# Whole-word float32 products for the first three units of two blocks, and VectorE and ScalarE ordered by hand at the start

## The chip, the cores and the metric

The kernel runs on one core of one Trainium2 chip. The metric is the device time of one execution in microseconds (us), here the median of three runs. TensorE does the matrix products, VectorE and ScalarE the elementwise work, GpSimd (POOL in the profile) more elementwise work, and SyncE's queue (SP) issues the transfers between HBM and the on-chip memory.

## The reference

There are two parts, and only the second one's result is returned. The first is a recurrent attention over 768 steps, for 4 batches of 8 heads of width 48:

```
cur   = u*k_t (outer) v_t
y_t   = r_t . (state + cur)
state = w_t * state + k_t (outer) v_t
```

The second is a feed-forward layer on the 3072 rows of 384 that come out of it: `h = x @ w_in` (384 to 2048), `g = h * cos(h)`, `out = g @ w_out` (2048 to 384). All data are float32.

## The kernel before, in words

The attention is cut into 24 chunks of 128 steps (4 batches, 6 chunks each), and two chunks make a block of 256 rows; `order` takes one chunk of every batch in turn. A chunk j goes through steps with one-letter names in the plan strings: `load` and `lv` (its transfers), `decay` (running products of the decays by two scans on VectorE, then r and k scaled by them), `diag` (the diagonal u terms, on TensorE for the first eight chunks), `a` (scores, masked into `asb` by VectorE), `t` and `s` (transposed k and the new state), `d` (the decayed state), `o` and `p` (the own and the past part of y) and `x` (y rounded into `xT`).

The feed-forward layer works on tiles f of 128 of the 2048 hidden columns, 16 in all. Two tiles make a unit of 512 columns of a PSUM bank (two tiles times 256 rows). For every unit and block `mm1` forms h, `gate` forms g on ScalarE, VectorE and GpSimd, and `mm2`, three units later, adds g times the output weights into the block's accumulators. The products run in float32r, a rounded form. To keep float32 accuracy each operand is split into a rounded high part and a low part (the rest), and a product is made of three passes, high by high, high by low and low by high (`PASSES`): 18 products for a unit's mm1, 12 for its mm2.

The weights come as 64-bit words and are made into float32 by `load_weights`: three casts on ScalarE (L163, L166, L167), a shift and an add on VectorE (L168, L169), the rounding to the high part on ScalarE (a cast at L141) and the low part on VectorE (a subtraction at L144). A tile holds its columns of w_in (kind 0) and rows of w_out (kind 1) side by side, so each of these steps covers 768 columns.

The raw words sit in the space of later tiles' weights (`RING`, five places): a raw transfer can start when the tile in its place has been cast.

The order: `START` is a list of steps for the first units, in which `f` is the transfer of a weight tile, `w` its conversion, `m0` and `m1` the two tiles of the next unit's mm1, and `mm2` the next mm2. `PAIR` says which of blocks 0 and 1 each of the first sixteen units belongs to: three units of block 0, three of block 1, then by turns. TensorE takes its instructions in the written order (`manual_schedule`). On all other engines a planner with its own estimates orders them, the written order being the priority. After `START`, `PLAN` gives a row of steps for every unit. `EARLY` and `LATER` say which engine does each kind of step.

Of the kernel before, what the change touches and what calls it, by code (L numbers as in the profile page):

```python
# [20 lines left out]
C = 128  # L21
# [13 lines left out]
BY_HAND = "P"  # L35
MERGE = 1
# [7 lines left out]
PASSES = ((0, 0), (0, 1), (1, 0))  # L44

LAG = 3
HP = 50
EARLY = dict(whole="p", rkt="v", cd="a", pc0="a", pc1="a", wadd="v", wm="a", whi0="a", whi1="a", ksh="a", gh="a", xh="a", rzh0="p", rzh1="v", r3="v", k3="v", rk="p", ru="p", rf0="v", rf1="v", kn="a", dd="v", rd0="a", rd1="a", rz0="v", rz1="v", ks="v", g0="p", g1="p", x="v", wlo0="v", wlo1="p", qf="s", qt="s", qr="s", qv="s", qx0="s", qx1="s", qo="s")
# [12 lines left out]
START = ["load0 load1 f lv0 decay0 f diag0 a0 lv1 decay1 diag1 a1 w load2 f w o0 x0 decay2 diag2 m0 m1",  # L61
# [10 lines left out]
def rwkv_cos_ffn(ctx: ExitStack, tc: tile.TileContext, tr, tn, tv, u, ut, wts, w, rkw, vst, us, xs, out):  # L72
# [80 lines left out]
    def load_weights(f):  # L153

        bits = raw.pop(f)
        wgt[f] = wt.tile([128, 2, 2, DM], F32R, tag=f"w{f}", name=f"w{f}")
        step = 2 if MERGE else 1
        for kind in range(0, 2, step):
            high, rest = wgt[f][:, kind:kind + step, 0], wgt[f][:, kind:kind + step, 1]
            words = bits[:, kind:kind + step].rearrange("p k (n w) -> p k n w", w=2)  # L160
            hi, lo = words[:, :, :, 1], words[:, :, :, 0]
            h = buf("h", [128, step, DM], I32)
            nc.scalar.activation(h.bitcast(F32), hi.bitcast(F32), AF.Copy, scale=2.0 ** -111)  # L163
            rest_of = buf("rd", [128, step, DM], I32)
            low16 = rest_of.bitcast(I16).rearrange("p k (n q) -> p k n q", q=2)
            nc.scalar.activation(low16[:, :, :, 0], lo.bitcast(U32), AF.Copy, scale=2.0 ** -29)  # L166
            nc.scalar.activation(low16[:, :, :, 1].bitcast(F16), hi.bitcast(F32), AF.Copy, scale=2.0 ** -60)  # L167
# [33 lines left out]
    def att_decay(a):  # L201

        if a["j"] < BY_PE:
            a["rkt"] = buf("rkt", [R, NP, C], F32)
            E["rkt"].tensor_tensor(out=a["rkt"], in0=a["r3"], in1=a["k3"], op=ALU.mult)  # L205
        wp = a["tt"][:, 1024:1024 + W129 + 1]
# [10 lines left out]
        E["r3"].tensor_tensor(out=a["r3"], in0=a["r3"], in1=a["pp"], op=ALU.mult)  # L217
        E["k3"].tensor_tensor(out=a["k3"], in0=a["k3"], in1=ee[:, :, 1:129], op=ALU.mult)
# [35 lines left out]
    def att_scores(a):  # L254
# [5 lines left out]
        for h in range(2):  # L260
            nc.vector.copy_predicated(a["asb", h], mask, pa[h])  # L261
# [91 lines left out]
    def gate(pool, ph, split=True):  # L353
# [7 lines left out]
        if not split:  # L361
            return rr
# [343 lines left out]
```

## Time and profile before

| | |
|---|---|
| median of 3 runs | 545.76 us (545.52 to 547.07) |
| the profiled execution | 547.09 us, its span 545.4 us |
| TensorE (PE) busy | 516.6 us, 95% of the span |
| VectorE (DVE) busy | 368.1 us, 68% |
| ScalarE (ACT) busy | 270.7 us, 50% |
| GpSimd (POOL) busy | 205.0 us, 38% |
| mean granted TensorE clock | 0.995 |

The span is the time from the first to the last instruction of one execution, which is run under the hardware profiler. Busy time counts instructions in progress. A row of the timeline gives the start, the duration and the engine, then the line of the kernel, the operation, what it writes and reads with the shapes, and how many instructions are merged into the row; in brackets stands the idle time of the engine before it and what ended this. PEld is TensorE's weight load. A line can be a helper's (L141 is every copy, L144 every low part).

### The profile page before, as it was taken

The numbers are of one execution on the slowest core, as the hardware profiler recorded it, in microseconds if no ns is written. First come the engines' busy times: TensorE is split into PE (matmuls) and PEld (weight loads), VectorE is DVE, ScalarE is ACT, GpSimd is POOL, SyncE is SP. The second block draws the span as 40 slices with busy tenths as digits, with TensorE's granted clock in tenths as the row PEclk, the third lists the DMA queues.
The fourth block names the chain that finished last, engine by engine and source line by source line (L and its number), as shares of the span: only waits on it lengthen the run. The fifth ranks groups of instructions, "written<-read, shape, count | busy, mean of one in ns | idle before, by whom it ended". The sixth has DMA issues, their size and how long they took to land. (4 is left out here: it accounts for less than half of the span.)

```text
span 545.4 us, 11929 instructions
## 1 busy us (share of the span) xinstructions
PE 516.6 (95%) x4980; PEld 492.9 (90%) x4980; DVE 368.1 (68%) x568; ACT 270.7 (50%) x456; POOL 205.0 (38%) x274
## 2 busy tenths in 40 slices
PE   3668999999899999999999999999999999999996
PEld 3666989989899999999999999999999999999996
DVE  7988999978787477478478478468468664433331
ACT  1778999645343444344444444344344345344542
POOL 4141336653344335335334334334334334323332
PEclk9999999999899999999999999999999999999999
DMA  8984771204370060061061051052032330000000
GB/s 269 277 303 167 240 220 41 77 7 132 117 180 16 30 183 12 30 171 25 30 170 26 30 150 46 30 148 48 29 106 99 131 131 1 31 1 1 30 2 31
DMA packets 16440, 51.38 MB, mean 94 GB/s; under 512 B 1984, under 2 KB 8384, under 8 KB 16384
## 3 DMA queue, kind: packets, MB, share of 16 engines
q1 hardware_dynamic: 16240, 50.49, 30.9%
q8 instruction: 40, 0.66, 0.5%
q14 instruction: 16, 0.13, 0.1%
q10 hardware_dynamic: 144, 0.10, 0.1%
HBM read 45.87 MB, written 4.72 MB: 93 GB/s over the span
## 5 line engine op out<-in xcount | busy, mean ns | idle before, releaser
L144 POOL TENSOR_TENSOR gs<-rr,gs 128x256 fp32r<-128x256 f32 x192 | 159.0, 850 | 228.3 <-ACT gs L141 220.1
L382 PE MATMUL ph<-xT,w 128*128 128x256 f32 x1728 | 225.2, 285 | 6.3 <-ACT w L141 4.8
L382 PEld LDWEIGHTS ph<-xT,w 128*128 128x128 f32 x1728 | 216.5, 192 | 9.8 <-ACT w L141 5.3
L401 PE MATMUL acc<-w,gs 128*128 128x384 f32 x1152 | 218.7, 339 | 1.0 <-DVE rr L360 1.0
L401 PEld LDWEIGHTS acc<-w,gs 128*128 128x128 f32 x1152 | 196.1, 188 | 4.6 <-issue 3.0
L359 ACT ACTIVATE rr<-rr,quarter 128x512 f32<-128x512 f32 x96 | 69.4, 723 | 110.2 <-DVE rr L358 110.0
L358 DVE SCALAR_TENSOR_TENSOR rr<-rr,ph 128x512 f32<-128x512 int32 x96 | 65.5, 682 | 76.2 <-ACT rr L357 63.3
L360 DVE TENSOR_TENSOR rr<-rr,ph 128x512 f32<-128x512 f32 x96 | 65.4, 682 | 46.8 <-ACT rr L359 46.8
L357 ACT ACTIVATE rr<-ph 128x512 int32<-128x512 f32 x96 | 57.1, 595 | 57.6 <-PE ph L382 57.4
L141 ACT CAST gs<-rr 128x512 fp32r<-128x512 f32 x96 | 59.0, 615 | 50.8 <-PE acc L401 40.3
L236 POOL TENSOR_SCALAR_AFFINE_SELECT asb<-cd 128x512 f32<-128x512 f32 x48 | 33.7, 733 | 50.6 <-ACT cd L141 25.6
L261 DVE COPY_PREDICATED asb<-mask,pa 128x512 f32<-128x512 uint8 x48 | 32.9, 735 | 5.8 <-PE pa L259 5.8
L259 PE MATMUL pa<-tt 48*128 48x128 f32 x384 | 32.6, 311 | 1.6 <-ACT ob L414 1.4
L259 PEld LDWEIGHTS pa<-tt 48*128 48x128 f32 x384 | 27.1, 210 | 6.8 <-issue 4.4
L208 DVE TENSOR_TENSOR_SCAN ee<-tt,one_e 112x516 f32<-112x516 f32 x24 | 31.4, 1308 | 1.8 <-DMA tt<-tr 1.8
L213 DVE TENSOR_TENSOR_SCAN tt<-tt,inj 112x516 f32<-112x516 f32 x24 | 31.3, 1303 | 0.1
L141 POOL COPY wholes<-ee 112x4 f32<-112x4 f32 x24 | 10.5, 438 | 54.1 <-DVE ee L208 54.1
L141 ACT COPY past<-dd 48x192 f32<-48x192 f32 x40 | 14.0, 351 | 21.9 <-DVE dd L249 21.3
L224 PEld LDWEIGHTS pc<-u_by_head,rkt 112*128 112x128 f32 x64 | 11.1, 259 | 14.8 <-DVE rkt L205 8.6
L224 PE MATMUL pc<-u_by_head,rkt 112*128 112x2 f32 x64 | 11.3, 299 | 13.6 <-DVE rkt L205 13.1
L217 DVE TENSOR_TENSOR tt<-tt 112x512 f32<-112x512 f32 x24 | 20.0, 833 | 0.1
L229 DVE TENSOR_TENSOR rk<-rk 128x384 f32<-128x384 f32 x16 | 10.9, 680 | 12.4 <-DMA rk<-tn 12.4
(65 smaller groups left out, 346.4 us busy)
## 6 DMA issues: line engine op xcount, KB each, us to landing
tt<-tr SPq DMA_DIRECT2D x22, 674.2 KB, 7.3
raw<-wts SPq DMA_DIRECT2D x16, 768.0 KB, 5.9
rk<-tn SPq DMA_DIRECT2D x16, 384.0 KB, 3.3
v<-tv SPq DMA_DIRECT2D x24, 224.0 KB, 7.0
ww<-w SPq DMA_DIRECT2D x6, 768.0 KB, 4.3
out<-ob SPq DMA_DIRECT2D x23, 192.0 KB, 2.0
tt<-tr SPq DMA_DIRECT2D x4, 224.0 KB, 4.3
tt<-tr SPq DMA_DIRECT2D x2, 226.2 KB, 3.5
```

Source lines behind the costliest of these rows:

```text
L141: (nc.scalar.copy if E[name] is nc.scalar else E[name].tensor_copy)(out=out, in_=in_)
L144: E[name].tensor_tensor(out=out, in0=full, in1=high.bitcast(F32), op=ALU.subtract)
L208: nc.vector.tensor_tensor_scan(out=ee.rearrange("p a t -> p (a t)")[:, ::-1], data0=wp[:, 1:W129 + 1][:, ::-1], data1=one_e.rearrange("p a ...
L236: nc.gpsimd.affine_select(out=asb, in_=col.unsqueeze(2).to_broadcast([C, NP, C]), pattern=[[0, 4], [1, C]], compare_op=ALU.is_equal, fill= ...
L259: nc.tensor.matmul(out=pa[h][:, p], lhsT=a["k3"][rows(h), p], rhs=a["r3"][rows(h), p], start=True, stop=True)
L261: nc.vector.copy_predicated(a["asb", h], mask, pa[h])
L357: nc.scalar.activation(nn, ph, AF.Copy, scale=INV2PI / W_SCALE, bias=0.25)
L358: nc.vector.scalar_tensor_tensor(out=rr, in0=nn, scalar=-2.0 * math.pi * W_SCALE, in1=ph, op0=ALU.mult, op1=ALU.add)
L359: nc.scalar.activation(rr, rr, AF.Sin, scale=1.0 / W_SCALE, bias=quarter)
L360: nc.vector.tensor_tensor(out=rr, in0=rr, in1=ph, op=ALU.mult)
L382: nc.tensor.matmul(out=ph[:, fi], lhsT=wgt[u * FU + fi][:, 0, a, kt * 128:(kt + 1) * 128], rhs=xT[:, b, kt], start=n == 0, stop=n == 3 * K ...
L401: nc.tensor.matmul(out=accs[i][j][:, :DM], lhsT=gs[:, a, fi, j * C:(j + 1) * C], rhs=wgt[u * FU + fi][:, 1, b], start=u == 0 and fi == 0 a ...
```

## The change

- For blocks 0 and 1, a unit of tiles below `WHOLE` (6, so units 0 to 2) forms mm1 by three float32 products per tile, of the whole weight words (`wholly`) and of x as float32 (`xfs`), instead of nine float32r products. The whole words lie in the space of later tiles' weights (8 to 10), x in that of tile 11.
- The split of these six tiles into high and low parts is a step of its own, `part_weights`, for w_in (`z` in the lists) and for w_out (`k`) separately. The high parts are ScalarE casts of 384 columns. The low part of w_in is VectorE's, that of w_out GpSimd's (`wlo0` and `wlo1` in `EARLY`). The split of x (`part_x`, `X`) is a step of its own as well.
- `START` is cut in two. In the first part VectorE and ScalarE also follow the written order, up to unit 2. Steps there can leave their later half for a place of its own: `later` keeps it under a name, and `!name` in the list (or `finish`) writes it out: `r` the f16 cast of a tile, `h` its shift and add, `y` the scaling of r and k by the decays, `c` the masked copies, `g` and `G` the two halves of a gate. In the second part (`START2`) only TensorE is by hand.
- The product r times k for the diagonal of chunks 0 and 1 moves behind the scans. The sine is applied once to a constant at the start.

```diff
-START = ["load0 load1 f lv0 decay0 f diag0 a0 lv1 decay1 diag1 a1 w load2 f w o0 x0 decay2 diag2 m0 m1",
-         "load3 f lv2 w f decay3 diag3 w m0 a2 m1 lv3 w f a3 o1 x2 w f m0 m1 mm2",
...
+START = ["load0 load1 f lv0 f decay0 !y0 diag0 a0 w !r0 lv1 load2 decay1 !y1 diag1 a1 w !r1 f load3 !c0 !h0 !c1 !h1 f w o0 x0 !r2 lv2 f w !r3 m0 m1",
+         "decay2 !y2 !h2 a2 decay3 !g0 !h3 f w !r4 !G0 lv3 m0 m1 f w !r5 !y3 diag3 !c2 a3 !g1 !c3 !h4 !G1 !h5 k0 k1 o1 x2 m0 m1"]
+START2 = ["k0 k1 k2 mm2 m0 m1 w f t0 t1 k3 mm2 m0 m1 s0 w f k4 k5 mm2 m0 m1 X0 z0 z1 w f load4 mm2 t2 t3 m0 m1 X1 z2 z3 w f s1 lv4",
+          "mm2 m0 m1 z4 z5 w f load5 mm2 m0 m1 w f decay4 lv5 mm2 m0 m1 w f diag4 decay5 mm2 a4 m0 m1 w f diag5 mm2 m0 m1 w a5 mm2 m0 m1 w load6 d4 d5",
...
+    nc.scalar.activation(cst.tile([128, 1], F32, name="first_sine"), quarter, AF.Sin)
...
+    def later(key, rest):
+
+        if by_hand[0]:
+            rests[key] = rest
+        else:
+            rest()
...
+    def part_weights(f, kind):
+
+        if f >= WHOLE or (f, kind) in parted:
+            return
+        finish("h%d" % f)
+        parted.add((f, kind))
+        if f not in wgt:
+            wgt[f] = wt.tile([128, 2, 2, DM], F32R, tag=f"w{f}", name=f"w{f}")
+        whole = wholly[f][:, f % 2, kind].bitcast(F32)
+        high, rest = wgt[f][:, kind, 0], wgt[f][:, kind, 1]
+        copy("whi%d" % kind, high, whole)
+        low_part("wlo%d" % kind, rest, whole, high)
...
+    def part_x(i):
+
+        xts[i] = xT = buf("xT", [128, 2, KT, BT], F32R)
+        copy("xh", xT[:, 0], xfs[i])
+        low_part("x", xT[:, 1], xfs[i], xT[:, 0])
...
+            if i < 2 and u * FU + fi < WHOLE:
+                for kt in range(KT):
+                    nc.tensor.matmul(out=ph[:, fi], lhsT=wholly[u * FU + fi][:, fi, 0, kt * 128:(kt + 1) * 128].bitcast(F32),
+                                     rhs=xfs[i][:, kt], start=kt == 0, stop=kt == KT - 1)
+                continue
...
+    with tc.manual_schedule(engines={ET.PE}):
+        by_hand[0] = True
+        with tc.manual_schedule(engines={ET.DVE, ET.Activation}):
+            first_order(START)
+        by_hand[0] = False
+        for key in list(rests):
+            finish(key)
+        first_order(START2)
```

## Rows read from the trace of the kernel before

**Rows 1.** Busy time by stretches: the stretch and its length in us, busy us and count of PE, PEld, DVE, ACT and POOL, then the granted TensorE clock, the DMA share and GB/s.

```profile
36.30:40.20 3.90, 0.00 (x0) 0.00 (x0) 3.90 (x5) 3.90 (x7) 2.49 (x2) 1.00 0.64 224
40.20:53.40 13.20, 10.68 (x107) 8.74 (x108) 11.91 (x18) 11.59 (x16) 2.82 (x3) 1.00 0.52 182
53.40:65.00 11.60, 11.60 (x109) 11.42 (x108) 11.08 (x16) 11.60 (x18) 2.00 (x4) 1.00 0.63 209
65.00:110.00 45.00, 42.96 (x346) 41.41 (x345) 45.00 (x63) 38.52 (x59) 26.75 (x23) 1.00 0.40 122
110.00:140.00 30.00, 29.02 (x329) 27.23 (x327) 24.45 (x38) 13.24 (x26) 13.14 (x17) 1.00 0.26 76
```

**Rows 2.** Timeline of the start, TensorE's first units and the first group of second products (L401).

```profile
25.58 4.19 PE L382 MATMUL ph<-xT,w 128*128 128x256 f32 x18
...
40.22 0.79 PE L382 MATMUL ph<-xT,w 128*128 128x256 f32 x2 [3.94 <-ACT w L141]
...
41.47 1.86 PE L382 MATMUL ph<-xT,w 128*128 128x256 f32 x7 [0.45 <-DVE w L144]
...
53.41 2.27 PE L401 MATMUL acc<-w,gs 128*128 128x384 f32 x12
```

**Rows 3.** The same timeline: ScalarE's three casts of a weight tile, and the load of the sine table.

```profile
14.13 0.90 ACT L163 ACTIVATE h<-raw 128x768 f32<-128x768 f32 x1
...
14.93 1.06 ACT L166 ACTIVATE rd<-raw 128x768 int16<-128x768 uint32 x1
...
15.86 1.06 ACT L167 ACTIVATE rd<-raw 128x768 f16<-128x768 f32 x1
...
33.40 1.28 ACT L359 ACT_TABLE_LOAD   x1
```

**Rows 4.** The same timeline: the masked copies, GpSimd's selects, add, x copies, shift, ScalarE's first gate step, VectorE's low part, VectorE's gate step, the sine and the gate's cast.

```profile
13.73 1.33 DVE L261 COPY_PREDICATED asb<-mask,pa 128x512 f32<-128x512 uint8 x2
...
14.30 1.23 POOL L236 TENSOR_SCALAR_AFFINE_SELECT asb<-cd 128x512 f32<-128x512 f32 x2 [2.14 <-ACT cd L141]
...
17.39 0.95 DVE L169 CUSTOM_DVE_ANT_0 h<-h,rd 128x1536 uint16<-128x1536 uint16 x1
...
20.15 0.83 ACT L141 CAST xT<-py 128x384 fp32r<-128x384 f32 x2
...
24.79 0.53 DVE L168 TENSOR_SCALAR h<-h 128x768 int32<-128x768 int32 x1
...
29.80 0.60 ACT L357 ACTIVATE rr<-ph 128x512 int32<-128x512 f32 x1 [0.56 <-PE ph L382]
30.08 0.94 DVE L144 TENSOR_TENSOR w<-h,w 128x768 fp32r<-128x768 f32 x1
...
30.95 0.67 DVE L358 SCALAR_TENSOR_TENSOR rr<-rr,ph 128x512 f32<-128x512 int32 x1
...
34.69 0.72 ACT L359 ACTIVATE rr<-rr,quarter 128x512 f32<-128x512 f32 x1
...
37.02 0.60 ACT L141 CAST gs<-rr 128x512 fp32r<-128x512 f32 x1
```

**Rows 5.** The issue of the raw transfers of weight tiles 2 and 3 (timeline of the start), and from the list of transfers issued between 7.1 and 7.9 and between 8.4 and 9 us: count, KB each, us from issue to landing.

```profile
7.20 0.71 SPq L151 DMA_DIRECT2D raw<-wts  x1
8.49 0.41 SPq L151 DMA_DIRECT2D raw<-wts  x1
...
raw<-wts SPq DMA_DIRECT2D x1, 768.0 KB, 14.0
...
raw<-wts SPq DMA_DIRECT2D x1, 768.0 KB, 18.5
```

**Rows 6.** Timeline, TensorE's rates: products at 46.97 and 48.31, and float32r groups and transpositions in the later stream.

```profile
46.97 0.64 PE L314 MATMUL py<-asb,v 128*32 128x128 f32 x4
48.31 0.52 PE L314 MATMUL py<-asb,v 128*32 128x128 f32 x10 [0.69 <-DVE asb L261]
...
102.32 2.35 PE L401 MATMUL acc<-w,gs 128*128 128x384 f32 x12
104.51 2.26 PE L382 MATMUL ph<-xT,w 128*128 128x256 f32 x18
106.61 2.25 PE L401 MATMUL acc<-w,gs 128*128 128x384 f32 x12
...
120.97 1.13 PE L268 MATMUL pt<-ident,tt 112*128 112x112 f32 x8 [0.55 <-DVE xT L144]
121.87 2.34 PE L382 MATMUL ph<-xT,w 128*128 128x256 f32 x18
```

**Rows 7.** GpSimd's low parts of the gate: grouped for 36 to 75 us and for 115 to 140 us (count, busy us, mean ns, idle before), and one pair from the timeline.

```profile
L144 POOL TENSOR_TENSOR gs<-rr,gs 128x256 fp32r<-128x256 f32 x10 | 12.1, 1228 | 24.6 <-ACT gs L141 24.6
...
L144 POOL TENSOR_TENSOR gs<-rr,gs 128x256 fp32r<-128x256 f32 x10 | 7.9, 808 | 11.4 <-ACT gs L141 11.4
...
64.89 2.90 POOL L144 TENSOR_TENSOR gs<-rr,gs 128x256 fp32r<-128x256 f32 x2 [2.88 <-ACT gs L141]
```

**Rows 8.** Two of TensorE's waits from its timeline, and the stretch behind the second (columns as in rows 1; the last but two is the granted clock).

```profile
69.35 2.15 PE L401 MATMUL acc<-w,gs 128*128 128x384 f32 x11 [0.96 <-DVE rr L360]
142.49 1.19 PE L259 MATMUL pa<-tt 48*128 48x128 f32 x14 [1.42 <-ACT ob L414]
...
143.00:147.00 4.00, 4.00 (x26) 3.84 (x25) 2.39 (x5) 0.48 (x1) 2.57 (x4) 0.57 0.85 238
```

More of the change, by code (lines that the diff above doesn't have):

```diff
@@ L155, in load_weights @@
         bits = raw.pop(f)
[L156 to L167, printed above, removed]
+        if f >= WHOLE:
+            wgt[f] = wt.tile([128, 2, 2, DM], F32R, tag=f"w{f}", name=f"w{f}")
+        elif f % 2 == 0:
+            wholly[f] = wholly[f + 1] = wt.tile([128, 2, 2, DM], I32, tag="w%d" % (8 + f // 2), name="whole")
@@ L174, in rwkv_cos_ffn @@
+    parted, wholly = set(), {}
     NB = NG // NCB
@@ L259, in att_scores, with masked @@
                 nc.tensor.matmul(out=pa[h][:, p], lhsT=a["k3"][rows(h), p], rhs=a["r3"][rows(h), p], start=True, stop=True)
-        for h in range(2):
-            nc.vector.copy_predicated(a["asb", h], mask, pa[h])
+        def masked():
+            for h in range(2):
+                nc.vector.copy_predicated(a["asb", h], mask, pa[h])
+        later("c%d" % a["j"], masked)
     def att_transpose(a):
@@ L287, in att_state, with taken, state_of @@
                                      rhs=a["v"][:, at:at + HD], start=True, stop=True)
+        def taken():
+            state_of(two, pst)
+        later("S%d" % i, taken)
+    def state_of(two, pst):
         for n, a in enumerate(two):
@@ L311, in att_own @@
             a = atts[i * BLK + n]
+            finish("c%d" % a["j"])
             for kt, p, h, q in LONG:
@@ L351, in check_decays, with gate @@
         nc.vector.tensor_tensor(out=wmax, in0=wmax, in1=top, op=ALU.max)
-    def gate(pool, ph, split=True):
+    def gate(pool, ph, split=True, t=None):
         rr = buf("rr", [C, FU, BT], F32, pool=pool)
@@ L357, in gate, with reduced, by_cosine @@
         nc.scalar.activation(nn, ph, AF.Copy, scale=INV2PI / W_SCALE, bias=0.25)
-        nc.vector.scalar_tensor_tensor(out=rr, in0=nn, scalar=-2.0 * math.pi * W_SCALE, in1=ph, op0=ALU.mult, op1=ALU.add)
-        nc.scalar.activation(rr, rr, AF.Sin, scale=1.0 / W_SCALE, bias=quarter)
-        nc.vector.tensor_tensor(out=rr, in0=rr, in1=ph, op=ALU.mult)
-        if not split:
-            return rr
-        gs = buf("gs", [C, 2, FU, BT], F32R, pool=pool)
-        copy("gh", gs[:, 0], rr)
-        for part in (slice(0, FU),) if E["g0"] is nc.vector else (slice(fi, fi + 1) for fi in range(FU)):
-            low_part("g0", gs[:, 1, part], rr[:, part], gs[:, 0, part])
-        return gs
+        def reduced():
+            nc.vector.scalar_tensor_tensor(out=rr, in0=nn, scalar=-2.0 * math.pi * W_SCALE, in1=ph, op0=ALU.mult, op1=ALU.add)
+            nc.scalar.activation(rr, rr, AF.Sin, scale=1.0 / W_SCALE, bias=quarter)
+            later("G%s" % t, by_cosine)
+        def by_cosine():
+            nc.vector.tensor_tensor(out=rr, in0=rr, in1=ph, op=ALU.mult)
+            if not split:
+                return
+            gs = buf("gs", [C, 2, FU, BT], F32R, pool=pool)
+            copy("gh", gs[:, 0], rr)
+            for part in (slice(0, FU),) if E["g0"] is nc.vector else (slice(fi, fi + 1) for fi in range(FU)):
+                low_part("g0", gs[:, 1, part], rr[:, part], gs[:, 0, part])
+            units[t] = gs
+        later("g%s" % t, reduced)
+        return rr
     def mm1(t, part=None):
@@ L385, in mm1 @@
         if part is None or part == FU - 1:
-            units[t] = gate(sb, ph)
+            gate(sb, ph, t=t)
     def mm2(t):
@@ L394, in mm2 @@
             accs[i] = [ps.tile([C, 512], F32, tag=x, name="acc") for x in tags]
+        finish("g%d" % t)
+        finish("G%d" % t)
         gs = units.pop(t)
+        for fi in range(FU):
+            part_weights(u * FU + fi, 1)
         todo = [(a, b, fi, j) for a, b in PASSES for fi in range(FU) for j in range(BLK)]
@@ L520, in rwkv_cos_ffn, with first_order @@
     engines(EARLY)
-    with tc.manual_schedule(engines={dict(P=ET.PE, S=ET.SP)[e] for e in BY_HAND}):
-        for row in START:
+    def first_order(rows):
+        for row in rows:
             for e in row.split():
```

82 lines of the change are left out of this document (69 added, 13 removed), and 3 rows, old and new, of the table START.

## The prediction, made before the change was run

> **What bounds the kernel now.** I read the page's engine shares and 40 slices first, then the chain of waits, then busy time by stretches, then the timeline of the start. TensorE is busy 95% of the span; VectorE 68%, ScalarE 50%, GpSimd 38%. The chain that ended last covers 0.2% of the span, two copies of the last output, and says only that the end follows TensorE. The stretches [rows 1] show where TensorE is not full: 3.90 us without any work at 36.3, 10.68 busy of 13.20 until 53.40, then 11.60 of 11.60, 42.96 of 45.00 and 29.02 of 30.00. So the time is the moment from which the stream is unbroken, 53.4, plus some 492 us in which little is idle. A change of the start can win only ahead of 53.4, and loses where it thins or lengthens what follows.
>
> The start in single groups [rows 2]: the first unit's 18 products run at 25.58; the second unit's second tile only at 40.22, 3.94 us late for ScalarE's rounding of the weights, and 0.45 late again at 41.47 for VectorE's low part; the first second-product group at 53.41. Two things in [rows 1] speak of the price later: VectorE is busy 45.00 of 45.00 from 65 to 110, GpSimd 26.75.
>
> **The change, part by part.**
>
> *First: when the second products begin.* The first three units now need only the whole words: per tile h, low half, f16 half on ScalarE, shift and add on VectorE, and x as it is. The roundings and low parts move behind. VectorE and ScalarE follow the written order, so I walk it. A tile's three ScalarE casts take 0.80 and 0.93 from start to start and 1.06 for the last, 2.8 us [rows 3]. VectorE's shift and add take 0.53 and 0.95, 1.45 together; a pair of masked copies 1.33; each of the gate's two VectorE steps 0.67; the gate's ScalarE steps 0.60, 0.72, 0.60; the two x copies 0.83 [rows 4].
>
> Up to 19 us the order is that of before. Then the landing of weight tiles rules: issued at 7.20 and 8.49, they land 14.0 and 18.5 us after issue, near 21.6 (the issue itself takes 0.71) and 27.0 [rows 5]. The queue ahead of them is in the same order, so I keep these. ScalarE, in order: tile 2 from 21.6; x copies behind its first two casts, done 24.2; tile 3 from 27.0 to 29.8. Unit 0 runs 24.2 to 29.8, as float32 at the slow rate (below); its gate opens 29.8 to 30.4. VectorE: gate step to 31.1, shift and add of tile 3 to 32.6. ScalarE: chunk 2's diagonal copy near 31.6, sine to 32.3, tile 4 to 35.1, cast of unit 0's gate to 35.7. TensorE: diagonals and scores of chunk 2, then unit 1 from 32.9. From here the TensorE's speed decides.
>
> What an f32 record costs: the trace has each float32 product as two records; a transposition's record of 112 columns starts 112 ns after the one before (8 in 0.90 from 120.97 to 121.87), by columns 257 ns for 256. The fp32r records of 256 columns start 117 ns apart (18 from 104.51 to 106.61), 0.46 a column, so the float32 record is about two such passes, 234 [rows 6]. Bounds 234 and 257 (one pass would be 117, which the 1.0 ns a column of the transpositions excludes); I take 234, 2.8 us for a unit's 12 records against 2.1. Early rows are twice as slow: 18 products in 4.19 at 25.58 [rows 2] against 2.26 at 104.51 [rows 6]. The granted clock is written 1.00 there too, but a duration near double is the lower of the two levels, 1.2 GHz. It ended between 46.97 (four records in 0.64) and 48.31 (ten in 0.52) [rows 6], after 7 us from 40.22 broken once by 0.45. In the new order TensorE works from 24.2 without a break into unit 1, so I take full speed from unit 1 on, though the stretch of units at 25.58, up to the stand at 36.3 [rows 1, 2], did not bring it; that is the other bound.
>
> At full speed unit 1 ends 35.7, its gate opens to 36.3. ScalarE then does tile 5 to 39.1 and only behind it chunk 3's diagonal copy, 39.3. GpSimd's two selects (1.23 the pair [rows 4]) end 40.5, the masked copy 41.25, shift and add of tile 4 42.7, gate step 43.4, tile 5 44.8. Unit 2's second tile ends 46.2. Against 53.4 that is -7.2. At the slow rate unit 1 ends 39.3, each later step 3.6 later, and with the last tile slow the end is 51.2: -2.2.
>
> *Second: GpSimd gets the low parts of the output weights.* Six instructions of 128x384 come to it, two ahead of each of the first three second products. Nearest rows are its 128x256 subtractions: 1228 ns from 36 to 75, 808 from 115 to 140 [rows 7]; 1.5 times that is 1.84 and 1.21. The stretch is the early one, so 1.84. Unit 1's gate is cast at 44.0 (43.4 and 0.60); its two low parts take 2.46 to 46.45, tile 0's 48.3, tile 1's 50.1. The second product starts 46.2, needs tile 1's low part for its seventh of 12 records, and ends 51.25 instead of 48.45: +2.8. With the fast rate +0.75; with the slowest pair, 2.90 at 64.89 [rows 7], 2.2 a tile and +4.0. For the next two groups: GpSimd has tile 2 and 3 done at 56.25 (behind the next gate's 2.46), TensorE asks at 56.0: +0.25. After that TensorE is later than GpSimd.
>
> The row shows GpSimd's instruction stretched from 808 to 1228 where VectorE is full [rows 7]. The Trainium skill (SBUF — State Buffer, Who interferes with whom) says a VectorE instruction with two SBUF inputs and a GpSimd instruction that reads SBUF exclude each other, the later one waiting for the whole of the other. The stretched rows agree with waiting. By the rule's full wait, one 0.94 subtraction of VectorE ahead of each GpSimd instruction, a gate's part would cost 0.81 plus 0.94, a tile 1.21 plus 0.94, the second product would end 52.9, and the sum would be 1.7 higher, on the way to the GpSimd rival below.
>
> *Third: three more units as float32.* Units 0 to 2 of block 1 run in the unbroken stream: 3 times 0.7, +2.1 (bound 2.9). The wait of 0.96 at 69.35 [rows 8] is for VectorE to free a bank that the unit before last wrote; a longer unit between eats 0.7 of it: -0.7 (0 to -0.96).
>
> *Fourth: what is put off.* VectorE later gets six halves of 0.47 and two x parts of 0.94 (from 0.94 for 128x768 [rows 4]), 4.7 us, and ScalarE twelve halves of 0.42 and two casts of 0.83. From 65 to 110 VectorE is full, yet not all of it is urgent (the decays of chunks 6 and 7 are taken up after 110, where it is busy 24.45 of 30.00 [rows 1]). TensorE idles 2.04 of these 45 us [rows 1], 0.96 of it in the one wait named. I take one more wait, somewhat shorter: +0.7. Bounds 0 and all 4.7. ScalarE, busy 38.52 of 45.00, hides its 6.7 us in the 6.5 idle and in TensorE's lead of some 4 us.
>
> *Small parts.* The sine table loaded at the start takes 1.28 us from ScalarE at 33.40 [rows 3]; in the walk ScalarE waits for a landing before and for TensorE after, so nothing. The product for the diagonals behind the scans moves 0.67 within VectorE's list: nothing. DMA: the raw buffers come free at ScalarE's last cast as before; the lists of loads move by a slot, while landings from 37 on were not waited for: nothing, up to 1 us if a transfer goes late.
>
> Sum: -7.2 + 2.8 + 0.25 + 2.1 - 0.7 + 0.7 = -2.05. The profiled execution took 547.09 with a span of 545.4; with the sum 545.0 and 543.4. It lies 1.3 above the median of 545.76, so for the runs: 543.7.
>
> **The rivals.**
>
> *The slow clock stays to unit 2, and the gain is eaten.* For it: the units from 25.58 on. Against: the float32 units are denser and nothing breaks them. Second product starts 51.2; GpSimd's chain shifts to tile 1 at 53.75, end 54.85 against 55.7: -0.8, then +0.25 + 2.1 - 0.7 + 0.7: +1.55, 547.3. No change, just.
>
> *GpSimd becomes the bound of the first three second products (slower).* At the slowest pair a unit's work on it is 2.9 and 4.4, 7.3 us, against TensorE's 5 to 6. The waits are 4.0, then about 1.4, then 1.2: 6.6 instead of 3.05, so +3.55. At 142.49 TensorE stood 1.42, and the four us behind it have a mean clock of 0.57 [rows 8], 1.7 us lost; a wait of 4 would bring that as well. -2.05 + 3.55 + 1.7 = +3.2, 549.0. It decides from about 2.0 us a tile on. For it: that pair of 2.90. Against: the walk leaves VectorE idle 2 us just there.
>
> *The stand at 142 goes.* ScalarE there has a sine queued ahead of the output copies that free the bank. A shifted plan may turn this order: 1.42 and 1.7 saved beyond the forecast, 540.6. Nothing in the change speaks of it.
>
> *It doesn't do what it says*: the written order itself stalls, a cast waiting for its landing ahead of x. The walk holds this (17 to 21.6 and 24.2 to 27.0 idle on ScalarE); no separate case.
>
> **How the numbers follow.** Forecast 0.42, slow clock 0.23, GpSimd 0.25, the stand 0.10. A measurement here tells 0.3%, 1.6 us. Faster: 0.33 of the forecast's (its own range is 542 to 545.5) and 0.10: 0.43. Same: 0.09 and 0.19 of the slow clock: 0.28. Slower: 0.04 and 0.25: 0.29. The range 540.0 to 548.2 holds the first two, the stand and the lower part of GpSimd's.
>
> **What would show it.** Right: records of L401's first group from about 46 with a wait inside it for GpSimd; unit records of about 234 ns in pairs for units 0 to 2 of both blocks; no table load at 33. The first step is wrong if that group begins past 49, or if unit 1's records are 450 ns apart. The second is wrong if no GpSimd wait stands there; the fourth if VectorE's waits in 65 to 110 exceed 3 us. The whole is wrong if TensorE's unbroken stream does not begin earlier than 52.

## The result and the profile after

The changed kernel takes 548.96 us (median of 7 runs, 548.09 to 552.92), the kernel before 546.24 beside it: a ratio of 1.0064, 95% interval 1.0037 to 1.0092. It is slower by 0.6%, where 543.7 was forecast. The profiled execution has a span of 547.3 us against 545.4. Its mean clock of 0.980 can't be held against the 0.995 of the profiled kernel before, whose slow start (18 products in 4.19 us [rows 2]) stands in the clock column as 1.00: the fourth run below has the same start, and there the column shows 0.50 from 21 to 48.

The shares of the whole hardly differ (page of the changed kernel):

```profile
PE 517.8 (95%) x4944; PEld 491.6 (90%) x4944; DVE 368.6 (67%) x566; ACT 271.1 (50%) x464; POOL 210.4 (38%) x280
```

Busy time by stretches (columns as in [rows 1]) shows where to look:

```profile
40.20:48.55 8.35, 5.69 (x48) 4.27 (x45) 5.68 (x9) 5.72 (x13) 4.90 (x6) 0.80 0.38 123
...
65.00:87.00 22.00, 21.01 (x175) 20.30 (x173) 21.95 (x32) 21.04 (x31) 10.29 (x9) 1.00 0.45 141
87.00:103.00 16.00, 12.86 (x72) 12.05 (x72) 15.86 (x19) 12.72 (x22) 7.99 (x9) 0.79 0.15 50
```

The stretch from 87 to 103 has 12.86 busy of 16.00 and a mean clock of 0.79. The kernel before was busy 42.96 of 45.00 around there, at 1.00 [rows 1].

The start, TensorE's units (L483), GpSimd's low part that ends the last wait, and the second products (L515), in the timeline:

```profile
22.44 2.86 PE L483 MATMUL ph<-xf,whole 128*128 128x256 f32 x12 [2.23 <-ACT xf L155]
27.11 1.56 PE L483 MATMUL ph<-xf,whole 128*128 128x256 f32 x6
34.03 2.93 PE L483 MATMUL ph<-xf,whole 128*128 128x256 f32 x6 [5.36 <-DVE whole L186]
...
44.37 4.54 PE L483 MATMUL ph<-xf,whole 128*128 128x256 f32 x12 [0.86 <-DVE whole L186]
48.56 2.75 PE L515 MATMUL acc<-w,gs 128*128 128x384 f32 x12
51.15 2.75 PE L483 MATMUL ph<-xf,whole 128*128 128x256 f32 x12
53.74 0.93 PE L324 MATMUL pt<-ident,tt 112*128 112x112 f32 x8
...
56.61 2.75 PE L483 MATMUL ph<-xf,whole 128*128 128x256 f32 x12
59.29 1.13 PE L342 MATMUL pst<-v,kn 128*64 128x48 f32 x32
...
62.27 1.31 PE L515 MATMUL acc<-w,gs 128*128 128x384 f32 x6 [0.60 <-POOL w L158]
```

The second products begin at 48.56, 4.85 us before those of [rows 2]. Behind that point the lead shrinks step by step: the fifth second product starts 2.2 us before the one of the kernel before (first row: the changed kernel, second row: the kernel before).

```profile
73.20 2.37 PE L515 MATMUL acc<-w,gs 128*128 128x384 f32 x12
...
75.38 2.36 PE L401 MATMUL acc<-w,gs 128*128 128x384 f32 x12
```

The loss stands between 87 and 103, in the timeline of the changed kernel with all engines:

```profile
86.12 0.95 PE L273 MATMUL pc<-u_by_head,rkt 112*128 112x2 f32 x8
86.93 2.33 PE L515 MATMUL acc<-w,gs 128*128 128x384 f32 x12
...
91.05 0.16 ACT L155 COPY cd<-pc 128x8 f32<-128x8 f32 x1
91.26 1.20 PE L310 MATMUL pa<-tt 48*128 48x128 f32 x14 [1.58 <-ACT cd L155]
91.34 3.23 DVE L244 TENSOR_TENSOR rkt<-tt 112x512 f32<-112x512 f32 x1
91.42 1.43 POOL L158 TENSOR_TENSOR gs<-rr,gs 128x256 fp32r<-128x256 f32 x2
...
92.39 3.85 PE L492 MATMUL ph<-xT,w 128*128 128x256 f32 x18
92.80 1.23 POOL L285 TENSOR_SCALAR_AFFINE_SELECT asb<-cd 128x512 f32<-128x512 f32 x2
94.49 0.67 DVE L450 SCALAR_TENSOR_TENSOR rr<-rr,ph 128x512 f32<-128x512 int32 x1
...
97.03 1.33 DVE L315 COPY_PREDICATED asb<-mask,pa 128x512 f32<-128x512 uint8 x2
97.80 1.05 PE L273 MATMUL pc<-u_by_head,rkt 112*128 112x2 f32 x8 [1.56 <-DVE asb L315]
...
107.92 2.26 PE L492 MATMUL ph<-xT,w 128*128 128x256 f32 x18
```

The diagonals of chunk 4 (`pc`) leave TensorE at 87.07. ScalarE copies them out (`cd`) at 91.05 only, behind five other steps that it began in between, and the scores (`pa`) stand 1.58 us for a bank that this copy frees. GpSimd's selects and VectorE's masked copies (L315) hang on it; these run at 97.03, behind L244 and four more steps, and the next `pc` stands 1.56. Behind each of the two stands the clock falls:

```profile
92.00:96.00 4.00, 4.00 (x24) 3.84 (x21) 4.00 (x4) 1.66 (x3) 2.03 (x4) 0.57 0.00 0
96.00:99.00 3.00, 1.44 (x12) 1.23 (x12) 3.00 (x6) 2.93 (x4) 0.59 (x1) 1.00 0.03 5
99.00:103.00 4.00, 4.00 (x17) 4.00 (x16) 3.86 (x6) 3.54 (x9) 4.00 (x4) 0.57 0.57 197
```

A group of 18 products takes 3.85 instead of 2.26. The two stretches of 4 us with a mean of 0.57 lose 2 times 4 times 0.43, 3.4 us, in this execution. The kernel before has the same lag, and covers it:

```profile
83.87 0.95 PE L224 MATMUL pc<-u_by_head,rkt 112*128 112x2 f32 x8
...
84.68 2.35 PE L401 MATMUL acc<-w,gs 128*128 128x384 f32 x12
...
87.58 2.34 PE L382 MATMUL ph<-xT,w 128*128 128x256 f32 x18 [0.56 <-DVE rr L360]
...
88.57 0.15 ACT L141 COPY cd<-pc 128x8 f32<-128x8 f32 x1
```

From the end of `pc` to `cd` it takes 3.75 us there (84.82 to 88.57) and 3.98 in the changed kernel. But before, two groups run on TensorE in that time, a second product and a unit; the second list of the changed kernel puts only one between `diag4` and `a4`. The two stands are 3.14 us where those of before are 0.56 and 0.52; with the clock that is 5.5, and it turns the lead of 2.2 into 3.4 behind (a unit that ran at 104.51 in [rows 6] runs at 107.92).

### The profile page after: what moved, and what is told of

Its sections match the earlier page's. It is cut to its first block, busy times and chain, and to the rows that moved or that the text cites. A ratio compares the mean times of both kernels' runs of the same rounds, so it can differ in the third digit from the quotient of the medians.

```text
span 547.3 us, 11874 instructions
## 1 busy us (share of the span) xinstructions
PE 517.8 (95%) x4944; PEld 491.6 (90%) x4944; DVE 368.6 (67%) x566; ACT 271.1 (50%) x464; POOL 210.4 (38%) x280
## 5 line engine op out<-in xcount | busy, mean ns | idle before, releaser
L158 POOL TENSOR_TENSOR gs<-rr,gs 128x256 fp32r<-128x256 f32 x192 | 156.1, 834 | 221.2 <-ACT gs L155 212.9
L515 PE MATMUL acc<-w,gs 128*128 128x384 f32 x1152 | 220.8, 341 | 0.6 <-POOL w L158 0.6
L492 PE MATMUL ph<-xT,w 128*128 128x256 f32 x1620 | 208.0, 284 | 0.0
L492 PEld LDWEIGHTS ph<-xT,w 128*128 128x128 f32 x1620 | 201.1, 191 | 2.3 <-issue 0.8
L515 PEld LDWEIGHTS acc<-w,gs 128*128 128x128 f32 x1152 | 197.4, 189 | 4.7 <-issue 2.0
L315 DVE COPY_PREDICATED asb<-mask,pa 128x512 f32<-128x512 uint8 x48 | 32.8, 734 | 7.5 <-PE pa L310 4.8
L310 PE MATMUL pa<-tt 48*128 48x128 f32 x384 | 31.2, 298 | 3.2 <-ACT cd L155 1.7
L310 PEld LDWEIGHTS pa<-tt 48*128 48x128 f32 x384 | 25.8, 199 | 8.2 <-issue 4.2
L483 PE MATMUL ph<-xf,whole 128*128 128x256 f32 x72 | 20.1, 435 | 8.5 <-DVE whole L186 6.2
L483 PEld LDWEIGHTS ph<-xf,whole 128*128 128x128 f32 x72 | 15.2, 218 | 12.1 <-DVE whole L186 7.1
```

Source lines behind the costliest of these rows:

```text
L158: E[name].tensor_tensor(out=out, in0=full, in1=high.bitcast(F32), op=ALU.subtract)
L310: nc.tensor.matmul(out=pa[h][:, p], lhsT=a["k3"][rows(h), p], rhs=a["r3"][rows(h), p], start=True, stop=True)
L483: nc.tensor.matmul(out=ph[:, fi], lhsT=wholly[u * FU + fi][:, fi, 0, kt * 128:(kt + 1) * 128].bitcast(F32), rhs=xfs[i][:, kt], start=kt == ...
L492: nc.tensor.matmul(out=ph[:, fi], lhsT=wgt[u * FU + fi][:, 0, a, kt * 128:(kt + 1) * 128], rhs=xT[:, b, kt], start=n == 0, stop=n == 3 * K ...
L515: nc.tensor.matmul(out=accs[i][j][:, :DM], lhsT=gs[:, a, fi, j * C:(j + 1) * C], rhs=wgt[u * FU + fi][:, 1, b], start=u == 0 and fi == 0 a ...
```

## The experiments

The kernel before ran beside each batch, with medians of 546.5 to 547.0; what counts is the ratio to it, with its 95% interval.

**One cause at a time.** Two things were suspected: the spacing of chunk 4's and 5's steps in the second list, and the put-off splits, which the planner puts between the hand-ordered steps (they are not hand-ordered themselves). The first run goes back to a wider spacing, the second ties the splits behind the hand-ordered ones by order alone, the third does both, and the fourth gives the kernel before the narrow spacing.

```diff
# e1_spacing
-mm2 m0 m1 w f decay4 lv5 mm2 m0 m1 w f diag4 decay5 mm2 a4 m0 m1 w f diag5
+decay4 mm2 m0 m1 w f lv5 diag4 mm2 m0 m1 w f decay5 a4 mm2 m0 m1 w f diag5
# e4_before_spaced
-mm2 m0 m1 w f decay4 mm2 m0 m1 w f diag4 mm2 m0 m1 w f decay5 a4 mm2 m0 m1 w f diag5
+mm2 m0 m1 w f mm2 m0 m1 w f decay4 mm2 m0 m1 w f diag4 decay5 mm2 a4 m0 m1 w f diag5
# e2_nohoist
+    def behind(inst):
+        if not by_hand[0] and inst.ins.engine in ends:
+            tc.add_manual_dep(inst.ins, ends[inst.ins.engine].name,
+                              mybir.DependencyInfo(mybir.DependencyClass.NoSync, mybir.DependencyReason.DATA), reason="order")
...
-        copy("whi%d" % kind, high, whole)
-        low_part("wlo%d" % kind, rest, whole, high)
+        behind(copy("whi%d" % kind, high, whole))
+        behind(low_part("wlo%d" % kind, rest, whole, high))
```

> The changed kernel with chunk 4's and 5's decay, diagonal and score steps put back to the places that they have among the units in the kernel before (two groups of products, not one, between a chunk's diagonal and its scores). Theory ORDER: the waits of 1.58 us at 91.26 and 1.56 at 97.80 are made by the written order, which leaves the diagonal's copy too little time; they go, and the clock with them stays at 1.00 from 90 to 104 (it was 0.50 for some 3.4 us twice): 1.58 + 1.56 + 1.7 + 1.7 = 6.5 less, about 542.5. Theory BACKLOG: VectorE and ScalarE are late in that stretch with the splits that were put off, whatever the order; the waits turn up at other products, 547 or more.

Measured: 545.12, ratio 0.9977 (0.9951 to 1.0003), between the two theories. The wait for `cd` is gone, the one for the masked copies is 1.92 now.

> The changed kernel in which the splits of weights and x of the second list can't be queued on VectorE or ScalarE ahead of the end of the first list (in the trace five subtractions of theirs and as many casts stand between the hand-ordered steps from 17 to 46 us). Theory HOIST: these delayed tile 3's add (33.02) and with it unit 1's second tile (34.03, 5.36 us late, clock 0.58 behind it); unit 1's second tile starts by 32 and the first second products by 46.5 instead of 48.56, 2 us gained, 547. Theory BACKLOG: what is gained there is lost from 60 to 105, where VectorE is full, and more waits appear: 549 to 552. If the landings of weight tiles rule the start, nothing moves: 549.

Measured: 544.80, ratio 0.998 (0.996 to 1.0). The second products begin at 45.08, 8.3 us before those of the kernel before; then TensorE stands 2.29 for a gate at 64.87 and 2.43 for `cd` at 90.60.

> Both edits together. ORDER and HOIST: the gains add, 6.5 and 2, about 540.5, below the kernel before. BACKLOG: 547 or more, since the splits then fall wholly into the stretch where VectorE is full.

Measured: 546.13, ratio 1.0006 (0.9981 to 1.0031). The start is 9.6 us earlier (43.77), and it is all given back: 2.28 at 63.55, 3.39 at 118.23 for the low part of the third block's x, each with a fall of the clock.

> The kernel before with only the places of decay4, diag4, decay5, a4, load6 among the units taken from the changed kernel's list (no float32 units, no splits put off, no order by hand on VectorE and ScalarE). ORDER: waits of 1 to 2 us ahead of chunk 4's scores and chunk 5's diagonal appear, each with a stretch of clock 0.50 behind it: 549 to 552. BACKLOG: there is none here, so no new waits, 546.

Measured: 547.43, ratio 1.0012 (0.9992 to 1.0032). It stands 1.47 for a gate at 87.67 and 0.97 for `cd` at 94.40, but loses nothing that can be told.

So either repair alone takes the loss away, and the two together don't add. Neither the spacing nor the place of the splits makes the loss by itself: the wide spacing with the splits between (first run), the narrow one with the splits behind (second) and the narrow one without any of the change (fourth) don't have it.

**Is it the amount of VectorE's work?** VectorE has next to no idle time from 60 to 110 in these versions. The fifth run leaves out the shift of the tiles from 7 on (4.95 us of VectorE; their weights are then other numbers), the eighth does the same to the kernel before, the sixth gives the kernel before as much more by doing that shift in two instructions, and the seventh moves low parts of w_in to GpSimd in the spaced version.

```diff
# e5_less_vector, e8_before_less_vector
-            nc.vector.tensor_scalar(out=h, in0=h, scalar1=3, scalar2=None, op0=ALU.logical_shift_left)
+            if f < 7:
+                nc.vector.tensor_scalar(out=h, in0=h, scalar1=3, scalar2=None, op0=ALU.logical_shift_left)
# e6_before_more_vector
-            nc.vector.tensor_scalar(out=h, in0=h, scalar1=3, scalar2=None, op0=ALU.logical_shift_left)
+            for by in (1, 2) if f > 6 else (3,):
+                nc.vector.tensor_scalar(out=h, in0=h, scalar1=by, scalar2=None, op0=ALU.logical_shift_left)
# e7_spacing_zpool
-wlo0="v", wlo1="p", wloz="v"
+wlo0="v", wlo1="p", wloz="p"
...
-        low_part("wlo%d" % kind, rest, whole, high)
+        low_part(("wloz", "wlo1")[kind], rest, whole, high)
```

> The changed kernel without the shift of the weight words of tiles 7 to 15 (nine VectorE instructions of 0.55, 4.95 us, all between 57 and 105 us; the words of these tiles are then wrong). It takes off VectorE there about what the put-off splits bring to it (six of 0.55 and two of 0.94, 5.2). Theory VECTOR: VectorE, full from 60 to 115, is the bound of that stretch, and every stand of TensorE in it is its lateness; the stands before 110 (4.7 us and 3.5 of clock in the changed kernel) mostly go: 541 to 543.5. Theory ORDER: they are made by where the list puts chunk 4's and 5's steps; they stay: 547 to 549.

Measured: 546.31, ratio 0.9987 (0.9968 to 1.0006), between the two: stands of 1.58 and 1.17 remain.

> The kernel before with that shift done in two instructions for tiles 7 to 15 (by 1 and by 2, the same result): 4.95 us more for VectorE in the same stretch, nothing else. VECTOR: TensorE gets stands of the size of the added work, less the 2.0 us it has now, and where one is longer than 1.4 the clock falls: 549 to 553. ORDER: the order of the list is that of before, so no new stands: 546 to 547.5.

Measured: 548.52, ratio 1.0031 (1.0015 to 1.0048): 1.6 us for 4.95 us of work, with a new stand of 2.81 at 121.14 for the low part of the third block's x. That the clock falls where a stand is longer than 1.4 is not borne out by the runs (last section).

> The changed kernel with chunk 4's and 5's steps in the places of before (the first experiment) and the low parts of w_in's splits on GpSimd instead of VectorE (six halves). VECTOR: 3.3 us less for VectorE in the start and up to 90, against GpSimd instructions of 1.2 to 1.8 each that hold VectorE's two-input instructions up: between nothing and 3 us under the first experiment's 545.1, 542 to 545. If GpSimd is late for a product instead: above 545.

Measured: 548.30, ratio 1.0011 (0.9982 to 1.0039). No better than the spaced version.

> The kernel before without the shift for tiles 7 to 15 (their words are then wrong): 4.95 us less for VectorE. VECTOR as the bound of this kernel too: its TensorE waits from 60 to 110 are 2.0 us, so at most 2 to 2.5 are gained: 544 to 545. If its stretch is TensorE's: 546 to 547.

Measured: 549.90, ratio 1.0062 (1.0041 to 1.0082): slower with less to do. The planner orders the queues anew, and TensorE stands 2.64 at 89.81 for a gate's last product, which has two scans ahead of it on VectorE (2.60 long at 83.68, 1.23 at 87.85).

More work cost something, less work cost more: the amount alone doesn't decide. The next runs test the order within the queues.

**Holding single steps.** From here a step that TensorE waits for is put ahead of less urgent steps in its queue, by ties of order as in the second run. The first hold: ScalarE does the rounding of tile 12, the second cast of tile 13, unit 8's gate cast and unit 9's first gate step only behind `cd` of chunk 4. The eleventh run, on the spaced version, holds chunk 5's product r times k and first scan behind chunk 4's masked copies instead (the tie as in the second hold below).

```diff
+    def behind_cd(key, inst=None):
+        if inst is not None:
+            held[key] = inst.ins
+        if key in held and 4 in first:
+            tc.add_manual_dep(held[key], first[4].name,
+                              mybir.DependencyInfo(mybir.DependencyClass.NoSync, mybir.DependencyReason.DATA), reason="order")
...
-            copy("cd", cd, pc)
+            i = copy("cd", cd, pc)
+            if a["j"] == 4:
+                first[4] = i.ins
+                for key in list(held):
+                    behind_cd(key)
```

> The changed kernel with ScalarE's copy of chunk 4's diagonals (cd) put ahead of the four steps of its queue that stood before it: the rounding of tile 12, the second cast of tile 13, the cast of unit 8's gate and the first gate step of unit 9 may only follow it (order alone, no wait on the chip). It ran at 91.05 though its products ended at 87.07, and TensorE stood 1.58 for it, then 1.56 for the masked copies that came of it, with two falls of the clock. QUEUE theory (the place of one small copy in an in-order queue made the loss): cd by 88.7, neither wait above 0.6 in 85 to 102, the first second product of unit 8 near 96.5 instead of 98.71, time 1.5 to 4 us under the changed kernel's: 545 to 547.5. BACKLOG theory (VectorE's work is late by then whatever stands in ScalarE's queue): another wait of 1.4 us or more within 20 us of there, on VectorE, and a time within 1 us of the changed kernel's, 548 to 550.

Measured: 547.78, ratio 1.0027 (1.0007 to 1.0046). The timeline:

```profile
89.58 0.17 ACT L155 COPY cd<-pc 128x8 f32<-128x8 f32 x1
...
89.80 1.16 PE L328 MATMUL pa<-tt 48*128 48x128 f32 x14 [0.34 <-ACT cd L155]
89.82 2.00 POOL L303 TENSOR_SCALAR_AFFINE_SELECT asb<-cd 128x512 f32<-128x512 f32 x2 [3.37 <-ACT cd L155]
90.27 1.05 DVE L258 TENSOR_TENSOR rkt<-tt 112x512 f32<-112x512 f32 x1
...
91.33 1.57 DVE L264 TENSOR_TENSOR_SCAN ee<-tt,one_e 112x516 f32<-112x516 f32 x1
...
96.27 1.33 DVE L333 COPY_PREDICATED asb<-mask,pa 128x512 f32<-128x512 uint8 x2
97.04 1.87 PE L287 MATMUL pc<-u_by_head,rkt 112*128 112x2 f32 x8 [3.78 <-DVE asb L333]
```

The first stand is 0.34 now, and the second 3.78. The selects end at 91.82, but the planner has put the scan of a later chunk (91.33) and four more steps ahead of the masked copies. The product of 112x512 (`rkt`) takes 1.05 here instead of the 3.23 of L244, and the copies are late all the same: its length isn't needed for the stand.

> The same hold on ScalarE's queue, put on the kernel whose split steps may only follow the hand-ordered ones. There TensorE stood 2.43 for cd at 90.60 and its next unit took 3.40 instead of 2.26. QUEUE: that stand goes, 2.43 and 1.1 saved, 541.0 to 542.5, faster than both kernels. BACKLOG: the stand moves to a VectorE step (the gate or the masked copies) and the time stays at 544 to 546.

Measured: 547.47, ratio 1.0031 (1.0011 to 1.005). `cd` runs at 89.08 and costs 0.84; the masked copies then cost 2.44.

> The kernel with the spread steps of chunks 4 and 5, where VectorE may do chunk 5's product r times k and its first scan only behind chunk 4's masked copies. There TensorE stood 1.92 for these copies at 92.93, and its next second product took 3.87 instead of 2.35. QUEUE: the stand goes, 1.92 and 1.5 saved, 541.5 to 543. BACKLOG: the scan comes later in its place, and TensorE stands for chunk 5's decays or for a gate, 544 to 546.

Measured: 549.97, ratio 1.0067 (1.0043 to 1.0091). The wait for the copies is gone; TensorE stands 0.81 for chunk 5's product, 1.99 ahead of its scores, and 3.19 for the low part of x at 123.87.

One hold moves the stand on, as the backlog theory has it, and none of the three gains anything that can be told on its kernel. But what stands ahead of the late step is again work for later. The second hold puts the masked copies of chunk 4 ahead of five steps on VectorE, the third the low part of the third block's x ahead of the scaling of chunk 7 and the diagonals of chunks 8 and 9:

```diff
# second hold; behind_copies and behind_low tie as above
-            later("l%d" % f, lambda: low_part("wlo0", rest, hf, high))
+            i = low_part("wlo0", rest, hf, high)
+            if f == 12:
+                behind_copies(i)
...
-                nc.vector.copy_predicated(a["asb", h], mask, pa[h])
+                i = nc.vector.copy_predicated(a["asb", h], mask, pa[h])
+            if a["j"] == 4:
+                copied[4] = i.ins
+                for inst in held2:
+                    behind_copies(inst)
# third hold
+            for inst in (E["rk"].tensor_tensor(out=rk, in0=rk, in1=a["rk"][:, 1], op=ALU.mult),
+                         E["ru"].tensor_tensor(out=rk, in0=rk, in1=u_sb, op=ALU.mult)):
+                if a["j"] < 10:
+                    behind_low(inst)
...
-                low_part("x", halves_of[:, 1, side], ys[side], halves_of[:, 0, side])
+                inst = low_part("x", halves_of[:, 1, side], ys[side], halves_of[:, 0, side])
+            if i == 2:
+                lowered[2] = inst.ins
+                for inst in held3:
+                    behind_low(inst)
```

> The kernel with cd put ahead on ScalarE, where VectorE also takes chunk 4's two masked copies ahead of five less urgent steps (the shift of tile 13, the low part of tile 12, the last gate product of unit 9, the first scans of chunks 6 and 7). With cd alone put ahead, its selects ended at 91.82, yet the masked copies ran at 96.27, behind two scans and four other steps, and TensorE stood 3.78. QUEUE (urgent steps stand behind less urgent ones in an in-order queue, and the work as such would fit): masked copies by 92.5, stands in 85 to 102 under 0.6 together, clock 1.00 there, the second product of unit 8 near 95, and 3 to 4.5 us below the kernel with cd alone: 543.0 to 545.0. BACKLOG (VectorE has too much before 120 in any order): the stand comes again on VectorE within 30 us, 2.5 us or more with its fall of the clock, 546.5 to 549.

Measured: 550.79, ratio 1.0066 (1.0042 to 1.0091). Between 85 and 117 there is one wait, of 0.33, and the clock is 1.00. Then:

```profile
115.62 2.25 PE L559 MATMUL acc<-w,gs 128*128 128x384 f32 x12
...
118.60 0.85 ACT L155 CAST xT<-py 128x384 fp32r<-128x384 f32 x2
119.70 0.53 DVE L313 TENSOR_TENSOR rk<-rk,u_sb 128x384 f32<-128x384 f32 x1
...
121.28 0.55 DVE L312 TENSOR_TENSOR rk<-rk 128x384 f32<-128x384 f32 x1
...
122.75 1.01 DVE L158 TENSOR_TENSOR xT<-py,xT 128x384 fp32r<-128x384 f32 x2
123.35 1.76 PE L362 MATMUL pt<-ident,tt 112*128 112x112 f32 x8 [5.48 <-DVE xT L158]
124.78 4.19 PE L536 MATMUL ph<-xT,w 128*128 128x256 f32 x18
```

ScalarE rounds x at 118.60; on VectorE the diagonals of chunks 8 and 9 (`rk`) and a scaling run first, and the low part of x follows at 122.75. TensorE stands 5.48, more than the two stands that were freed.

> The same two holds on the kernel whose split steps follow the hand-ordered ones. There cd alone left TensorE 2.44 for the masked copies at 95.17. QUEUE: that stand goes with 0.5 to 1 of clock behind it, and 2.4 to 3.5 us are saved against the kernel with cd alone: 544.0 to 545.1. BACKLOG: the stand returns near 120, for the low part of x that the next block waits for (it stood 1.03 there), 546.5 to 548.

Measured: 547.27, ratio 1.0007 (0.9989 to 1.0026). The same stand, 2.57 at 118.84.

> The kernel with split steps behind the hand-ordered ones and both holds, and a third hold: VectorE scales chunk 7's r and k and forms the diagonals of chunks 8 and 9 only behind the low part of block 2's x. There these steps stood ahead of it from 114.7 on, the low part ran at 118.25 though its rounding was done near 115.1, TensorE stood 2.57 and the next two groups took 4.19 and 2.66 instead of 2.35 and 2.25. ORDER (the stands come from the order of VectorE's queue): the low part before 116.5, no stand above 0.5 in 85 to 140, 2.57 and 2.2 saved: 542.0 to 543.5, below both kernels. BACKLOG (VectorE is still too far behind): a stand of 1.4 or more for chunk 7's steps or a gate before 140, 546 to 548.

Measured: 541.15, ratio 0.9903 (0.9879 to 0.9926). This is faster than both kernels. The same place:

```profile
114.23 0.85 ACT L155 CAST xT<-py 128x384 fp32r<-128x384 f32 x2
114.73 1.02 DVE L158 TENSOR_TENSOR xT<-py,xT 128x384 fp32r<-128x384 f32 x2
...
116.34 2.35 PE L566 MATMUL ph<-xT,w 128*128 128x256 f32 x18
```

The low part follows its rounding at once, the unit behind it runs at 116.34 instead of 121.87 [rows 6], and no stand is left there. Nor is one near 142: the largest behind it is 0.64, at 127.27. Not all of the gain is the place that the third hold ties. Between the profiled executions of the thirteenth and this run, 4.3 us are there at the second product of 134.20 (138.47 in the thirteenth) and 6.2 at the next one: in between the stand of 1.42 near 142 is gone, for output copies of ScalarE that no hold ties (it is gone in the second and third run too). A stand of 2.26 for a gate is left at 63.86.

> The same third hold on the changed kernel with both holds. There the low part ran at 122.75, the rounding of x at 118.60, and TensorE stood 5.48, its next group 4.19 instead of 2.35. ORDER: the low part near 119.6, since its rounding on ScalarE stays behind two gates; the stand falls to about 2.3: 547 to 548. BACKLOG: the stand stays above 4, 549.5 to 551.

Measured: 544.12, ratio 0.996 (0.994 to 0.9979), less than expected: the stand is 1.55, with no fall of the clock behind it, and the one near 142 is gone. The changed kernel itself, then, is faster than the kernel before once three places in its queues are held.

> The kernel before with the three holds alone, none of the change: it tells whether the 1% below the kernel before is the change's, once the queues are held, or the holds' own. HOLDS ALONE: 541 to 543, as with the change. CHANGE: the kernel before stands only 0.55 for the low part of x at 120.97 and 0.52 for the masked copies at 95.94, so the holds find at most 1 to 1.5 us there, more only if the stand of 1.42 at 142.49 goes by the shift as well (3.1 with its clock): 543.5 to 547.

Measured: 545.73, ratio 0.9988 (0.9967 to 1.0009). The holds alone give nothing that can be told. The fourteenth run lies clear of this interval; the fifteenth overlaps it.

> The kernel with spread steps and the split steps behind the hand-ordered ones, with the third hold alone (chunk 7's scaling and the diagonals of chunks 8 and 9 behind the low part of block 2's x). It started the second products 9.6 us before the kernel before, had no stand between 66 and 112, and then stood 3.39 at 118.23 for that low part, with 3.82 for the next group instead of 2.35; time 546.13. ORDER: that stand and its clock go, 3.4 and 1.5 saved: 540.5 to 542.5. BACKLOG: they come back before 145: 545 to 547.

Measured: 542.70, ratio 0.9934 (0.9909 to 0.996), against 1.0006 of the third run without it. The stand is not gone, 1.54 at 116.77, but no fall of the clock follows it.

The instructions are the same with and without the holds, on each engine as many; order alone makes 1.0064 into 0.996 (all three holds), and the third hold alone makes 1.0066 into 0.996, 1.0007 into 0.9903 and 1.0006 into 0.9934. So the loss was one of order: in ScalarE's and VectorE's queues, and in TensorE's list that leaves them more or less time (the first run). Each tie also lets the planner order the rest anew, as near 142; what part of a gain is the tied place alone was read from single traces. Why the planner orders as it does was not measured.

## Why the prediction was wrong

*First step (-7.2).* Right in kind and over-sized: -4.85. The walk took VectorE and ScalarE to follow the written order alone. The planner put split steps between, on VectorE for instance

```profile
28.20 0.93 DVE L158 TENSOR_TENSOR xT<-xf,xT 128x768 fp32r<-128x768 f32 x1
...
29.13 1.28 DVE L158 TENSOR_TENSOR w<-whole,w 128x384 fp32r<-128x384 f32 x1
...
33.02 0.96 DVE L186 CUSTOM_DVE_ANT_0 whole<-h,rd 128x1536 uint16<-128x1536 uint16 x1
...
45.77 0.95 DVE L186 CUSTOM_DVE_ANT_0 whole<-h,rd 128x1536 uint16<-128x1536 uint16 x1
```

so that the add of tile 3 (L186) ends at 33.98 instead of 32.6 and that of tile 5 at 46.72 instead of 44.8. Tile 5's lateness, 1.9, is most of the 2.35 missing, and some of it is the clock's: unit 1's second tile took 2.93, where its first took 1.56. Where splits come behind (e2), the start is 8.3 earlier, so the put-between steps and what followed from them were worth 3.5. The clock came neither as forecast (slow in unit 0, full from unit 1 on) nor by the other bound: unit 0 took 2.86, full speed; unit 1's second tile was slow behind a stand of 5.36; the clock was back at 1.00 from 38 to 44 and fell again behind stands of 1.60 and 0.86, so that unit 2 took 4.54.

*Second step (+3.05).* Over-sized: some 0.5 within the first group, which takes 2.75 instead of 2.27 [rows 2], none in the second, 0.60 in the third (62.27), about 1.1. GpSimd's 128x384 low parts took 1.33 us on average between 40 and 60, where 1.84 was taken.

*Third step (+2.1 - 0.7).* The rate was a little over-sized: at full speed a record starts 216 ns after the one before (2.59 for the 12 from 51.15), where 234 was taken. From start to start the three units are 2.59, 2.68 and 2.40, so 1.4 together over 2.1 each. The wait of 0.96 at 69.35 [rows 8] is gone, as forecast, but one of 0.99 for ScalarE's copies of k stands at 72.14, and nothing is gained.

*Fourth step (+0.7).* This step failed. It priced the put-off work by its amount, took "one more wait, somewhat shorter" on VectorE, and put ScalarE's part at nothing. Within 60 to 110 VectorE got only 2.0 us of put-off work (two halves of 0.55, one x part of 0.94), all before 74. What came was 5.5 us: two stands and their clock between 87 and 103, where none of the put-off work stood, the first of them for a copy of ScalarE. The forecast had the row that bore on it, VectorE busy 45.00 of 45.00 [rows 1], and read it as a store of work in which some waits. It was a queue in order, as the holds show: steps that TensorE waited for stood behind steps that could wait. That TensorE's earlier arrival and the narrower list made them late, where they had been just in time (0.56 and 0.52 before), is argued from the first, second and fourth run.

*Small parts.* The table load is gone from 33, as said. "The product for the diagonals ... moves: nothing" holds as far as the rows show.

*Rivals.* None named this. The GpSimd rival came out near in time (549.0) by luck: GpSimd's waits were about 1.1. Its price of a stand, the stand and 1.7 of clock, held for the two stands here, though not for every stand in the other runs (below). The stand at 142 stayed, 1.43 at 144.93. No sign of being wrong fired as it was written: the nearest, "VectorE's waits in 65 to 110 exceed 3 us", counted VectorE alone, to which 1.56 of the 3.14 was put down; unit 1's second tile had its records 427 ns apart, for the 450 of another.

## What to carry to other kernels

Where an engine that feeds the bound one is busy all through a stretch, a lead gained ahead of it may be worth nothing by itself: look for what each feeding step has behind and ahead of it in its queue, and how much time the bound engine's own groups give it. When a stand moves on under a repair, read what ran ahead of the late step; if that is work for later, it is order and not amount, and a tie of order on that one step tells. Such a stand can be paid twice, by its length and by the clock behind it.

## What the runs showed of the hardware

- Whether the clock fell behind a stand of TensorE of up to 2.3 us could not be told from the stand. Where it fell, the column shows 0.50 for over three us, some 1.7 us lost, or for about twice as long. From 50 us on, in the traces of all versions, it fell behind all nine stands of 2.43 us and more, behind five of the eight from 1.9 to 2.3, and behind eight of the eighteen from 1.42 to 1.58. The stand near 142, of 1.42 or 1.43, brought a fall in six traces and none in six. No fall followed 1.55 in the fifteenth run (first two rows); in the fourteenth one came at 128.7, behind stands of 0.35 and 0.64 (last two rows), and in the second at 132.0, behind 0.25 and 0.18. So the 1.7 of clock is at best an even chance for a stand of 1.4 to 1.6, and each profile is one execution.

```profile
118.87 1.13 PE L376 MATMUL pt<-ident,tt 112*128 112x112 f32 x8 [1.55 <-DVE xT L158]
119.76 2.34 PE L554 MATMUL ph<-xT,w 128*128 128x256 f32 x18
...
127.27 1.16 PE L368 MATMUL pa<-tt 48*128 48x128 f32 x14 [0.64 <-ACT cd L155]
128.35 3.91 PE L589 MATMUL acc<-w,gs 128*128 128x384 f32 x12
```

- One VectorE product of 112x512 (L244) took 3.23 us at 91.34, beside GpSimd's low parts and selects from 91.42 to 94.03, where it takes 0.68 in the start of the same run (19.69). The Trainium skill (SBUF — State Buffer, Who interferes with whom) says that a VectorE instruction with two SBUF inputs contends with a GpSimd instruction that reads SBUF, for ports that are an exclusive lock. The rows fit such a wait of VectorE, since the product ends at 94.57, 0.54 after the last of GpSimd's, though its own start is written 0.08 ahead of theirs. The late masked copies stood behind it in the queue; in the ninth run it took 1.05 and they were late as well.
- Less work can be slower: without the shift of nine tiles the kernel before took 0.6% more, since the order of the queues changed with it.
